# One PSUM bank moved from the down projection to the convolution, results taken out one operation at a time, and other shares of work per unit

## The chip, the cores and the metric

The kernel runs on one core of one Trainium2 chip. The metric is device time in microseconds (us) of one execution, as a median of several; executions of one kernel agree here within about 0.2% (0.34% in one run). The engines are PE (matmul), PEld (its weight loads), DVE (vector), ACT (scalar), POOL (GpSimd) and SP, which only issues transfers. PSUM is the memory that PE writes its results to; the kernel uses it as eight banks.

## The reference

```python
h_filt = (np.maximum(pos_emb @ w1, 0.0) @ w2) * np.exp(-0.01 * pos)[:, None]
u = x * v                                        # (4, 12480, 128)
y = irfft(rfft(u, 2*S) * rfft(h_filt, 2*S))[:, :S]   # a causal convolution per channel
t = (x * y).reshape(49920, 128)
h = t @ w_in                                     # 128 -> 2048
return (h * np.cos(h)) @ w_out                   # 2048 -> 128
```

All is float32. The long convolution is done as matmuls in two passes there and two back.

## The kernel before

A convolution of one batch element has five stages. **u** forms x times v and its sums and differences, without PE. **f1** and **f2** are the two transforms there, and f2's result is multiplied with the filter's spectrum. **i1** and **i2** are the two transforms back. Every stage is a Python generator of "units" (30 in u, 64 in f1, 48 in f2, 64 in i1, 30 in i2). A unit's matmuls go to a PSUM bank, and `after` takes the bank's content out one unit later:

```python
    def units(n, steps, before, mm, after, ahead=2):
        for j in range(min(ahead, n)):
            before(j)
        last = None
        for j in range(n):
            if j + ahead < n:
                before(j + ahead)
            now = mm(j)
            if last is not None:
                after(j - 1, last)
            last = now
            yield steps
        after(n - 1, last)
        yield REST

    U_STEPS, F1_STEPS, F2_STEPS, I1_STEPS, I2_STEPS = 2.1, 1.2, 2.3, 1.2, 1.6

    def f2_product(pool, ps, h, k1):
        ...
        for r, op in ((0, ALU.subtract), (1, ALU.add)):
            nc.vector.tensor_tensor(y[:, r], uu[:, 0], hh[:, r], op=ALU.mult)
            nc.vector.tensor_tensor(t[:, r], uu[:, 1], hh[:, 1 - r], op=ALU.mult)
            nc.gpsimd.tensor_tensor(y[:, r], y[:, r], t[:, r], op=op)

    def u_multiply(tiles, engine):
        xt, vt = tiles
        engine.tensor_tensor(xt[:, :, :], xt[:, :, :], vt[:, :, :], op=ALU.mult)

    def u_sums(u, tiles, a):
        ...
        for place, op, e in ((a, ALU.add, nc.gpsimd), (ODD + a, ALU.subtract, nc.vector)):
            e.tensor_tensor(u[...], below, above, op=op)
```

The cosine layer runs in 1664 "steps" (104 tiles of 480 tokens, 16 chunks of hidden width each). A step is an up matmul into bank `ph`, then a (ACT), k (DVE), f (POOL), cs (ACT), gt (DVE), then a down matmul that adds into bank `acc`. The down matmul trails by four steps. The first convolution runs alone at the start; the other three are threaded into the first 1140 steps, each unit being given its number of steps:

```python
        ps_acc = ctx.enter_context(tc.tile_pool(name="ps_acc", bufs=2, space=PSUM))
        ps_h = ctx.enter_context(tc.tile_pool(name="ps_h", bufs=4, space=PSUM))
        ps_c = ctx.enter_context(tc.tile_pool(name="ps_c", bufs=2, space=PSUM))
        ...
        for i in range(len(steps) + LAG):
            if i < len(steps):
                ...
                hidden[i] = moe_up(mpool, n, c)               # PE, ACT a, DVE k, POOL f
            if 0 <= i - 1 < len(steps):
                gates[i - 1] = moe_act(mpool, *hidden.pop(i - 1))   # ACT cs, DVE gt
            if i >= LAG:
                moe_down(pn, pc, gates.pop(i - LAG))          # PE
                if pc == NFC - 1:
                    ots[pn] = moe_evict(mpool, pn)            # ACT ot <- acc
            ...
            owed += share
            while owed > 0.0:
                owed -= next(conv, owed)                      # units of the convolution
```

## Time and profile before

| | before |
|---|---|
| median (runs) | 4256.94 us (4256.48 to 4257.34) |
| start, until the first up matmul | 635 us |
| steps with three convolutions threaded in | 2742 us |
| steps alone (tail), to the last up matmul | 874 us |

The three parts are read from the profiled execution, whose span was 4262.5 us; 11 us follow the last up matmul.

Three of the page's costliest groups: line, engine, operation, output from inputs, shapes and count, then busy time and mean ns of one, then idle time just before them and what ended it.

```profile
L578 POOL TENSOR_TENSOR f<-a,k 128x480 f32<-128x480 f32 x1664 | 2021.9, 1218 | 1174.9 <-DVE k L575 1174.9
L569 PE MATMUL ph<-at,w_in_sb 128*128 128x480 f32 x3328 | 1647.4, 577 | 102.6 <-DVE gt L585 101.6
L369 POOL TENSOR_TENSOR slots<-slots,t 120x256 f32<-120x256 f32 x384 | 296.6, 795 | 228.2 <-DVE t L368 176.6
```

PE waits 102 us at the up matmul for gt, which frees a ph bank. POOL waits for DVE's products of f2 (t, L368) for 177 us. Both waits belong to the threaded stretch or the start; the tail has no gap.

Throughout this document a stage's **loss** is its length minus what its matmuls cost PE back to back. I count the matmuls in the stage's stretch and take 0.4007 us for each of the two instructions of an up or down matmul, 0.161 in f1, 0.2135 in f2, 0.1005 in i1, 0.107 in i2, and 0.11 for a transpose. These are start-to-start times in full stretches of the timeline; the medians over the whole trace are up to 3% higher, which would take some 12 us off the sum. In the tail the same costs leave 3 us of 874. A loss holds both PE's waits and the time lost while the granted clock was low. It is read from one profiled execution of each kernel. Over three convolutions the kernel before loses u 122, f1 21, f2 123, i1 22, i2 14 us.

### The profile page before, as it was taken

Reading aid. Unit: us, or ns where it says so; the run is one execution under the profiler, and the core shown is the slowest. Engines: PE = TensorE matmul, PEld = TensorE weight load, DVE = VectorE, ACT = ScalarE, POOL = GpSimd, SP = SyncE. Lnnn points to the kernel's source line nnn. Section 1 sums busy time; section 2 is a strip of 40 time slices with the busy share of each in tenths; the row PEclk is TensorE's granted clock in tenths of the full one; section 3 lists DMA queues with packets and bytes.
Section 4 is the critical chain, followed back from the end, with each engine's and each line's share of the span. In section 5 each row is a group of like instructions: output and inputs, shape, how many; then the busy total and the mean of one; then the engine's idle time right before and its main releaser. Section 6 shows DMA issues by size and latency. Waiting matters only on the chain.

```text
span 4262.5 us, 49170 instructions
## 1 busy us (share of the span) xinstructions
PE 3916.4 (92%) x13882; PEld 2244.3 (53%) x13882; DVE 3047.8 (72%) x6588; ACT 2415.2 (57%) x4484; POOL 2546.8 (60%) x2311
## 2 busy tenths in 40 slices
PE   5868778999999998998899989988999999999999
PEld 3836673554456653554466634644466644444444
DVE  8657669987778568777776588766675566666666
ACT  1343155775567445655455456644554577777777
POOL 2422347657865457568854476568754577777776
PEclk8557889999999999999999999999999999999999
DMA  3354343112211442012201531022103400000000
GB/s 86 89 167 120 96 136 106 50 52 78 82 51 42 142 142 85 15 50 81 75 12 51 177 112 42 15 73 78 52 15 107 127 19 19 19 19 19 19 19 14
DMA packets 271763, 293.63 MB, mean 69 GB/s; under 512 B 16741, under 2 KB 204101, under 8 KB 271237
## 3 DMA queue, kind: packets, MB, share of 16 engines
q1 hardware_dynamic: 271493, 290.50, 23.6%
q8 instruction: 112, 1.84, 0.2%
q14 instruction: 158, 1.29, 0.1%
HBM read 210.12 MB, written 80.31 MB: 68 GB/s over the span
## 4 chain that ended last, share of the span: by engine, by line
PE 65%; POOL 11%; DVE 10%; ACT 5%; DMA 5%; issue 3%; SPq 0%; DVEq 0%; POOLq 0%; ACTq 0%
PE ph L569 24%; PE acc L591 23%; POOL f L578 6%; POOL slots L369 5%; PE cv L404 4%; PE cv L386 4%; ACT cs L583 3%; PE cv L343 3%; PE ps L343 3%; DVE gt L585 2%; DMA w<-wd 2%; DMA hd<-h 2%; PE ph L116 2%; DVE slots L336 1%; PE ps L386 1%
## 5 line engine op out<-in xcount | busy, mean ns | idle before, releaser
L578 POOL TENSOR_TENSOR f<-a,k 128x480 f32<-128x480 f32 x1664 | 2021.9, 1218 | 1174.9 <-DVE k L575 1174.9
L569 PE MATMUL ph<-at,w_in_sb 128*128 128x480 f32 x3328 | 1647.4, 577 | 102.6 <-DVE gt L585 101.6
L591 PE MATMUL acc<-gt,w_out_sb 128*128 128x480 f32 x3328 | 1618.0, 568 | 0.5 <-DVE gt L585 0.5
L572 ACT ACTIVATE a<-ph,quarter 128x480 f32<-128x480 f32 x1664 | 1094.2, 658 | 750.7 <-PE ph L569 691.8
L585 DVE TENSOR_TENSOR gt<-ph,cs 128x480 f32<-128x480 f32 x1664 | 1091.7, 656 | 476.3 <-ACT cs L583 452.7
L583 ACT ACTIVATE cs<-f 128x480 f32<-128x480 f32 x1664 | 998.4, 600 | 690.6 <-POOL f L578 688.7
L575 DVE TENSOR_SCALAR k<-a 128x480 f32<-128x480 f32 x1664 | 778.8, 468 | 528.3 <-ACT a L572 514.4
L591 PEld LDWEIGHTS acc<-gt,w_out_sb 128*128 128x128 f32 x3328 | 633.8, 190 | 715.5 <-issue 713.5
L569 PEld LDWEIGHTS ph<-at,w_in_sb 128*128 128x128 f32 x3328 | 584.8, 191 | 575.4 <-issue 290.4
L369 POOL TENSOR_TENSOR slots<-slots,t 120x256 f32<-120x256 f32 x384 | 296.6, 795 | 228.2 <-DVE t L368 176.6
L357 PE MATMUL ps<-slots,w 124*120 124x256 f32 x384 | 165.9, 576 | 80.7 <-DVE w L250 45.6
L386 PEld LDWEIGHTS cv<-cs,slots 120*96 120x96 f32 x1536 | 180.5, 168 | 82.0 <-issue 72.1
L357 PE MATMUL cv<-slots,w 124*120 124x256 f32 x576 | 155.3, 390 | 49.7 <-PE acc L591 36.0
L404 PEld LDWEIGHTS cv<-slots,tm 96*104 96x104 f32 x1440 | 173.1, 171 | 46.7 <-issue 36.0
L386 PE MATMUL cv<-cs,slots 120*96 120x120 f32 x1536 | 191.2, 267 | 3.3 <-POOL slots L369 3.3
L404 PE MATMUL cv<-slots,tm 96*104 96x128 f32 x1440 | 178.7, 275 | 11.0 <-DMA tm<-td 7.2
L343 PEld LDWEIGHTS cv<-c,slots 104*124 104x124 f32 x768 | 130.6, 192 | 84.4 <-issue 54.8
L357 PEld LDWEIGHTS ps<-slots,w 124*120 124x120 f32 x384 | 93.0, 268 | 153.0 <-issue 70.5
L357 PEld LDWEIGHTS cv<-slots,w 124*120 124x120 f32 x576 | 98.7, 182 | 134.3 <-PE acc L591 78.0
L343 PE MATMUL cv<-c,slots 104*124 104x192 f32 x768 | 159.5, 330 | 3.2 <-POOL slots L336 2.6
L396 DVE TENSOR_TENSOR slots<-cv,other 96x240 f32<-96x240 f32 x384 | 135.9, 393 | 0.5
L330 POOL TENSOR_TENSOR xt<-xt,vt 104x512 f32<-104x512 f32 x30 | 38.3, 1276 | 137.5 <-DMA vt<-in_v_dram 127.0
(111 smaller groups left out, 2781.8 us busy)
## 6 DMA issues: line engine op xcount, KB each, us to landing
h<-hd SPq DMA_DIRECT2D x192, 240.0 KB
tm<-td SPq DMA_DIRECT2D x90, 312.0 KB
xt<-in_x_dram SPq DMA_DIRECT2D x120, 208.0 KB
vt<-in_v_dram SPq DMA_DIRECT2D x120, 208.0 KB
xs<-in_x_dram SPq DMA_DIRECT2D x120, 208.0 KB
zd<-zs SPq DMA_DIRECT2D x120, 208.0 KB
zb<-zd SPq DMA_DIRECT2D x104, 240.0 KB
out_dram<-ob SPq DMA_DIRECT2D x104, 240.0 KB
```

The source lines that it names most:

```text
L343: nc.tensor.matmul(ps[0:KE, i * 2 * N1:(i + 1) * 2 * N1], u[:, b, 0:KE, i], c1[0:u.shape[0], :, :].rearrange("p r k -> p (r k)"), start=Tr ...
L357: nc.tensor.matmul(ps[0:N2, i * 2 * D:(i + 1) * 2 * D], w[:, i, :], parts[0:KE, :, k1 + i, :, :], start=True, stop=True)
L369: nc.gpsimd.tensor_tensor(y[:, r], y[:, r], t[:, r], op=op)
L386: nc.tensor.matmul(ps[0:N1, (i * 2 + r) * N2:(i * 2 + r + 1) * N2], parts[0:N2, r, :, b, i], cs[:, r:r + 2, :].rearrange("p c a -> p (c a) ...
L404: nc.tensor.matmul(ps[0:R, i * D:(i + 1) * D], t[:, i, r, :], slots[0:N1, :, place, :], start=(r == 0), stop=(r == 1))
L569: nc.tensor.matmul(ph[:, 0:TOK], w_in_sb[:, c * P:(c + 1) * P], ats[n][:, :], start=True, stop=True)
L572: nc.scalar.activation(a[:, :], ph[:, 0:TOK], AF.Identity, bias=quarter[:, 0:1], scale=INV_TWO_PI)
L575: nc.vector.tensor_scalar(out=k[:, :], in0=a[:, :], scalar1=ROUND, scalar2=ROUND, op0=ALU.add, op1=ALU.subtract)
L578: nc.gpsimd.tensor_tensor(f[:, :], a[:, :], k[:, :], op=ALU.subtract)
L583: nc.scalar.activation(cs[:, :], f[:, :], AF.Sin, scale=TWO_PI)
L585: nc.vector.tensor_tensor(gt[:, :], ph[:, 0:TOK], cs[:, :], op=ALU.mult)
L591: nc.tensor.matmul(accs[n][:, 0:TOK], w_out_sb[:, c, :], gt[:, :], start=(c == 0), stop=(c == NFC - 1))
```

## The change

It is meant to let PE run on while results are taken out. The convolution gets a third bank, paid for by the second bank of the down sums; in the tail, where the convolution banks lie idle, odd tiles borrow one. The results of a unit are no longer taken out in one burst: `after` is a generator now, and each of its pieces is followed by a share of a unit's steps; a unit's matmuls are issued in two halves as well. u and f2 get more steps per unit, f1 and i1 fewer. Two copies out of PSUM move from DVE to ACT, and every third row of a table is made with POOL. The transposes of a tile move, so that four of them stand between the last down matmul of one tile and the first of the next.

```diff
-    def units(n, steps, before, mm, after, ahead=2):
+    def units(n, steps, before, mm, after, parts, ahead=2):
...
-            now = mm(j)
-            if last is not None:
-                after(j - 1, last)
-            last = now
-            yield steps
-        after(n - 1, last)
+            now = None
+            for i in range(parts):
+                if i == 0 or 2 * i == max(parts, 2):
+                    now = mm(j, now, min(i, 1))
+                if i == 0 and parts == 1:
+                    now = mm(j, now, 1)
+                next(last, None)
+                yield steps / parts
+            next(last, None)
+            last = after(j, now)
+        for _ in last:
+            pass
         yield REST
...
-    U_STEPS, F1_STEPS, F2_STEPS, I1_STEPS, I2_STEPS = 2.1, 1.2, 2.3, 1.2, 1.6
+    U_STEPS, F1_STEPS, F2_STEPS, I1_STEPS, I2_STEPS = 2.75, 0.8, 2.9, 0.8, 1.6
...
             nc.vector.tensor_tensor(y[:, r], uu[:, 0], hh[:, r], op=ALU.mult)
+            yield
             nc.vector.tensor_tensor(t[:, r], uu[:, 1], hh[:, 1 - r], op=ALU.mult)
             nc.gpsimd.tensor_tensor(y[:, r], y[:, r], t[:, r], op=op)
+            yield
...   (the same in f1_evict, i1_evict, i2_out and filter_keep; u multiplies in two halves)
-        nc.vector.tensor_copy(out=at[:, :], in_=pt[:, 0:TOK])
+        nc.scalar.copy(out=at[:, :], in_=pt[:, 0:TOK])
...   (the same for ob; the transposes move to other steps of a tile)
-            accs[n] = ps_acc.tile([P, BANK], F32, name="acc")
+            accs[n] = bank() if ready == B - 1 and n % 2 else \
+                ps_acc.tile([P, BANK], F32, name="acc")
...
-        ps_acc = ... bufs=2 ...
+        ps_acc = ... bufs=1 ...
-        ps_c = ... bufs=2 ...
+        ps_c = ... bufs=3 ...
```

More of the change, by code (lines that the diff above doesn't have):

```diff
@@ L268, in make_t, with make_third @@
              tw_t[:, 1, n2:n2 + 1], **how)
+    def make_third(pool, t, n2, half=None):
+        if n2 % 3 < 2:
+            make_t(t, n2, half=half)
+        else:
+            spare = pool.tile([N1, 2, R], F32, name="spare")
+            make_t(t, n2, spare=spare[:, :, :])
     ROWS = 8
@@ L326, in u_load, with u_multiply @@
         return tiles
-    def u_multiply(tiles, engine):
+    def u_multiply(tiles, half, engine):
         xt, vt = tiles
-        engine.tensor_tensor(xt[:, :, :], xt[:, :, :], vt[:, :, :], op=ALU.mult)
+        engine.tensor_tensor(xt[:, half, :], xt[:, half, :], vt[:, half, :], op=ALU.mult)
     def u_sums(u, tiles, a):
@@ L337, in u_sums, with f1_mm @@
                             below, above, op=op)
-    def f1_mm(ps, u, b):
-        for i in range(2):
-            nc.tensor.matmul(ps[0:KE, i * 2 * N1:(i + 1) * 2 * N1], u[:, b, 0:KE, i],
-                             c1[0:u.shape[0], :, :].rearrange("p r k -> p (r k)"),
-                             start=True, stop=True)
+    def f1_mm(ps, u, b, i):
+        nc.tensor.matmul(ps[0:KE, i * 2 * N1:(i + 1) * 2 * N1], u[:, b, 0:KE, i],
+                         c1[0:u.shape[0], :, :].rearrange("p r k -> p (r k)"),
+                         start=True, stop=True)
     def f1_evict(ps, b):
@@ L350, in f1_evict, with f2_mm @@
         nc.vector.tensor_copy(out=parts[ODD:KE, 0, :, b, :], in_=pj[ODD:KE, 1])
+        yield
         nc.vector.tensor_scalar(out=parts[ODD:KE, 1, :, b, :], in0=pj[ODD:KE, 0],
                                 scalar1=-1.0, scalar2=None, op0=ALU.mult)
-    def f2_mm(ps, w, k1):
-        for i in range(2):
-            nc.tensor.matmul(ps[0:N2, i * 2 * D:(i + 1) * 2 * D], w[:, i, :],
-                             parts[0:KE, :, k1 + i, :, :], start=True, stop=True)
+        yield
+    def f2_mm(ps, w, k1, i):
+        nc.tensor.matmul(ps[0:N2, i * 2 * D:(i + 1) * 2 * D], w[:, i, :],
+                         parts[0:KE, :, k1 + i, :, :], start=True, stop=True)
     def f2_product(pool, ps, h, k1):
@@ L367, in f2_product @@
             nc.vector.tensor_tensor(y[:, r], uu[:, 0], hh[:, r], op=ALU.mult)
+            yield
             nc.vector.tensor_tensor(t[:, r], uu[:, 1], hh[:, 1 - r], op=ALU.mult)
             nc.gpsimd.tensor_tensor(y[:, r], y[:, r], t[:, r], op=op)
+            yield
     def filter_keep(pool, ps, h, k1):
@@ L380, in filter_keep, with i1_mm @@
                     in1=h[:, g, r, :], op0=ALU.mult, op1=ALU.add)
+            yield
         nc.sync.dma_start(hd[k1 // 2, :, :, :, :], h[:, :, :, :])
-    def i1_mm(ps, b):
-        for i in range(2):
-            for r in range(2):
-                nc.tensor.matmul(
-                    ps[0:N1, (i * 2 + r) * N2:(i * 2 + r + 1) * N2],
-                    parts[0:N2, r, :, b, i],
-                    cs[:, r:r + 2, :].rearrange("p c a -> p (c a)"), start=True, stop=True)
+    def i1_mm(ps, b, i):
+        for r in range(2):
+            nc.tensor.matmul(
+                ps[0:N1, (i * 2 + r) * N2:(i * 2 + r + 1) * N2],
+                parts[0:N2, r, :, b, i],
+                cs[:, r:r + 2, :].rearrange("p c a -> p (c a)"), start=True, stop=True)
     def i1_evict(pool, ps, b):
@@ L397, in i1_evict, with i2_mm @@
                                     other[:, :, :], op=op)
-    def i2_mm(ps, t, g):
-        for i in range(G):
+            yield
+    def i2_mm(ps, t, g, part):
+        for i in range(part * G // 2, (part + 1) * G // 2):
             n2 = g * G + i
@@ L415, in i2_out @@
         nc.sync.dma_start(zd[b, :, g * G:(g + 1) * G, :], zs[:, :, :])
-    def units(n, steps, before, mm, after, ahead=2):
+        yield
+    def units(n, steps, before, mm, after, parts, ahead=2):
         for j in range(min(ahead, n)):
             before(j)
-        last = None
+        last = iter(())
         for j in range(n):
@@ L445, in before, with after, mm @@
                 tiles[j] = u_load(pool, bufs, b, j * UA)
-            def mm(j):
-                u_multiply(tiles[j], engine)
-                return tiles.pop(j)
+            def after(j, _):
+                for half in range(2):
+                    u_multiply(tiles[j], half, engine)
+                    yield
+                u_sums(u, tiles.pop(j), j * UA)
+                yield
             clear_gap(u)
-            yield from units(H // UA, U_STEPS, before, mm,
-                             lambda j, t: u_sums(u, t, j * UA), ahead=bufs - 2)
+            yield from units(H // UA, U_STEPS, before, lambda j, ps, i: None, after, 3,
+                             ahead=bufs - 2)
     def f1_units(bank, u):
-        def mm(j):
-            ps = bank()
-            f1_mm(ps, u, j)
+        def mm(j, ps, i):
+            if i == 0:
+                ps = bank()
+            f1_mm(ps, u, j, i)
             return ps
-        return units(CB, F1_STEPS, lambda j: None, mm, lambda j, ps: f1_evict(ps, j))
+        return units(CB, F1_STEPS, lambda j: None, mm, lambda j, ps: f1_evict(ps, j), 2)
     def f2_units(bank, use, make=None):
@@ L479, in before, with mm @@
                     nc.sync.dma_start(hs[j][:, :, :, :], hd[j, :, :, :, :])
-            def mm(j):
-                ps = bank()
-                f2_mm(ps, ws.pop(j), 2 * j)
+            def mm(j, ps, i):
+                if i == 0:
+                    ps = bank()
+                f2_mm(ps, ws[j], 2 * j, i)
                 return ps
             yield from units(N1 // 2, F2_STEPS, before, mm,
-                             lambda j, ps: use(pool, ps, hs.pop(j), 2 * j))
+                             lambda j, ps: use(pool, ps, hs.pop(j), 2 * j),
+                             4 if use is f2_product else 2)
     def i1_units(bank):
         with tc.tile_pool(name="mid", bufs=2) as pool:
-            def mm(j):
-                ps = bank()
-                i1_mm(ps, j)
+            def mm(j, ps, i):
+                if i == 0:
+                    ps = bank()
+                i1_mm(ps, j, i)
                 return ps
             yield from units(CB, I1_STEPS, lambda j: None, mm,
-                             lambda j, ps: i1_evict(pool, ps, j))
+                             lambda j, ps: i1_evict(pool, ps, j), 2)
     def i2_units(bank, b, make=None):
@@ L512, in before, with mm @@
                                   block(x, b, slice(j * G, (j + 1) * G)))
-            def mm(j):
-                ps = bank()
-                i2_mm(ps, ts.pop(j), j)
+            def mm(j, ps, i):
+                if i == 0:
+                    ps = bank()
+                i2_mm(ps, ts[j], j, i)
                 return ps
             yield from units(N2 // G, I2_STEPS, before, mm,
-                             lambda j, ps: i2_out(pool, ps, xss.pop(j), b, j))
+                             lambda j, ps: i2_out(pool, ps, xss.pop(j), b, j), 2)
     def t_units():
@@ L527, in t_units @@
                 for i in range(G):
-                    make_t(t[:, i, :, :], g * G + i)
+                    make_third(pool, t[:, i, :, :], g * G + i)
                     yield
@@ L535, in conv_units @@
         keep = t_units() if b == 1 else iter(())
-        for steps in f1_units(bank, slots[0:R, :, :, :]):
-            next(keep, None)
+        for i, steps in enumerate(f1_units(bank, slots[0:R, :, :, :])):
+            if i % 2:
+                next(keep, None)
             yield steps
         yield from f2_units(bank, f2_product)
-        for steps in i1_units(bank):
-            next(keep, None)
+        for i, steps in enumerate(i1_units(bank)):
+            if i % 2:
+                next(keep, None)
             yield steps
@@ L603, in moe_store @@
         ob = pool.tile([N2, TOK // N2, D], F32, name="ob", bufs=1)
-        nc.vector.tensor_copy(out=ob[:, :, :].rearrange("i m d -> i (m d)"),
-                              in_=pt[0:N2, :])
+        nc.scalar.copy(out=ob[:, :, :].rearrange("i m d -> i (m d)"), in_=pt[0:N2, :])
         nc.sync.dma_start(
@@ L667 @@
             for j, _ in enumerate(f1_units(bank, slots[0:FR, :, :, :])):
-                if j % 4 == 3:
+                if j % 8 > 4:
                     next(first_u, None)
@@ L671 @@
                     bank, filter_keep, lambda w, k1: make_w(w, k1, half=bank))):
-                if j % 3 == 2:
+                if j % 2:
                     next(first_u, None)
@@ L690 @@
             with tc.tile_pool(name="spare", bufs=2) as pool:
-                def make(t, n2):
-                    if n2 % G < G - 1:
-                        make_t(t, n2, half=bank)
-                    else:
-                        spare = pool.tile([N1, 2, R], F32, name="spare")
-                        make_t(t, n2, spare=spare[:, :, :])
-                for _ in i2_units(bank, 0, make):
+                for _ in i2_units(bank, 0, lambda t, n2: make_third(pool, t, n2, bank)):
                     pass
-        ps_acc = ctx.enter_context(tc.tile_pool(name="ps_acc", bufs=2, space=PSUM))
+        ps_acc = ctx.enter_context(tc.tile_pool(name="ps_acc", bufs=1, space=PSUM))
         ps_h = ctx.enter_context(tc.tile_pool(name="ps_h", bufs=4, space=PSUM))
-        ps_c = ctx.enter_context(tc.tile_pool(name="ps_c", bufs=2, space=PSUM))
+        ps_c = ctx.enter_context(tc.tile_pool(name="ps_c", bufs=3, space=PSUM))
         mpool = ctx.enter_context(tc.tile_pool(name="moe", bufs=2))
@@ L747 @@
             if i < len(steps):
-                if c == LAG + 1 and n - 1 in ots:
+                if c == LAG - 1 and n + 1 < NALL:
+                    moe_turn(mpool, n + 1)
+                if c == NFC // 2 and n - 1 in ots:
                     moe_store(mpool, n - 1, ots.pop(n - 1))
-                if c == NFC // 2 and n + 1 < NALL:
-                    moe_turn(mpool, n + 1)
             owed += share
```

## The prediction

> **What bounds the kernel now.** The page comes first, and in it the strip of slices: how busy each engine is along the run.
>
> ```profile
> PE   5868778999999998998899989988999999999999
> DVE  8657669987778568777776588766675566666666
> POOL 2422347657865457568854476568754577777776
> PEclk8557889999999999999999999999999999999999
> ```
>
> Slices are 107 us. Up to slice 6 (about 640 us) the filter and the first convolution run; then come 1664 "steps" of the cosine layer (up matmul, a, k, f, cs, gt, down matmul), with convolutions 1 to 3 threaded into the first 1140 of them, and the last 524 alone. PE is at 9 everywhere but in dips that come three times. To name them I asked for busy time in stretches of 100 us; columns: PE, PEld, DVE, ACT, POOL, granted clock, DMA share, GB/s.
>
> ```profile
> 1300.00:1400.00 100.00, 100.00 (x478) 62.79 (x477) 80.38 (x191) 69.39 (x152) 50.61 (x42) 1.00 0.15 41
> 1600.00:1700.00 100.00, 82.01 (x208) 34.48 (x206) 90.18 (x139) 53.78 (x94) 76.09 (x66) 1.00 0.29 88
> 1900.00:2000.00 100.00, 90.64 (x264) 46.23 (x264) 71.14 (x162) 48.80 (x85) 81.69 (x80) 1.00 0.30 82
> 3500.00:3600.00 100.00, 100.00 (x270) 48.35 (x269) 69.65 (x128) 76.55 (x126) 72.56 (x61) 1.00 0.06 15
> ```
>
> The first line is stage i1 and the last is the tail: PE full. The second is stage u (x times v, sums and differences), the third stage f2 (product with the filter). Only these two leave PE free.
>
> How much they lose: the tail runs 481 steps in 800 us (count of f in the groups of that stretch), so a step with its share of transposes costs PE 1.663 us. By the starts in the timeline, one f1 unit adds 0.65 us of PE, f2 0.85, i1 0.80, i2 1.71. Cutting the run where matmuls of one source line stop and the next begin, stage u of convolution 2 (1550 to 1694 us) holds 63.5 steps: 144 minus 106 leaves 38 us lost; f2 (1866 to 2130) holds 112 steps and 48 units: 264 minus 186 minus 41 leaves 37. Over three convolutions u loses about 118 us, f2 126 (40, 37, 49), and f1, i1, i2 together some 50, of which perhaps half is error of my unit costs. The prize is therefore at most 250 to 290 us, 6 to 7%.
>
> Why u loses: the timeline of DVE there,
>
> ```profile
> 1599.20 0.85 DVE L330 TENSOR_TENSOR xt<-xt,vt 104x512 f32<-104x512 f32 x1
> 1599.97 0.95 DVE L336 TENSOR_TENSOR slots<-xt 104x256 f32<-104x256 f32 x1
> 1600.84 0.40 DVE L575 TENSOR_SCALAR k<-a 128x480 f32<-128x480 f32 x1
> 1601.16 0.65 DVE L585 TENSOR_TENSOR gt<-ph,cs 128x480 f32<-128x480 f32 x1
> 1601.73 1.05 DVE L575 TENSOR_SCALAR k<-a 128x480 f32<-128x480 f32 x1
> ```
>
> and of POOL:
>
> ```profile
> 1599.46 1.17 POOL L336 TENSOR_TENSOR slots<-xt 104x256 f32<-104x256 f32 x1
> 1601.32 1.20 POOL L578 TENSOR_TENSOR f<-a,k 128x480 f32<-128x480 f32 x1 [0.68 <-DVE k L575]
> 1602.86 1.20 POOL L578 TENSOR_TENSOR f<-a,k 128x480 f32<-128x480 f32 x1 [0.35 <-DVE k L575]
> 1604.02 1.18 POOL L336 TENSOR_TENSOR slots<-xt 104x256 f32<-104x256 f32 x1
> ```
>
> k takes 0.40 us when POOL is still and 1.05 when POOL runs f; DVE's L336 takes 0.41 or 0.95 likewise. They take turns. One unit with two steps lasts 4.56 us (1599.46 to 1604.02), all of it turns of f, k, multiply (0.53 undisturbed), add on POOL (0.66) and subtract (0.33). So a step costs this turn-taking 1.51 us (4.56 minus 1.52, halved) and the unit 1.5.
>
> Why f2 loses: there DVE does four products in one burst, and the waits show PE held at its next convolution matmul (the releaser printed is PE's own older matmul; the products' end fits, 1959.27 against a start at 1959.36).
>
> ```profile
> PE cv L357 <- PE acc L591: 12.1, 17, 0.8
> PE ph L569 <- DVE gt L585: 10.5, 14, 1.1
> ```
>
> [...] 0.40 against 1.05 us above; gt, with an input in PSUM, keeps 0.65. [...]
>
> **The change part by part.**
> (1) Third convolution bank, and DVE's operations handed out one per chunk. It aims at f2. Before, a steady f2 unit takes 50 us/9.3 units = 5.38 us against 4.68 of PE (2.3 x 1.663 + 0.85). Turn-taking would allow about 2.3 x 1.51 + 2 x 0.69 = 4.85 (0.69 is my estimate of L369 without k's share, on the line through f, 480 elements in 1.20, and L255, 208 in 0.62); so 0.5 us per unit is burst and bank wait. After, with 2.9 steps, PE needs 4.82 + 0.85 = 5.67 and turn-taking 2.9 x 1.51 + 1.38 = 5.76. Adding 0.1 to 0.3 us of remaining disorder, a unit loses 0.2 to 0.4 us: 29 to 58 us for 144 units, against 144 x 0.70 = 101 before. Saved: 43 to 72, say 62.
> (2) u gets 2.75 steps for 2.1. PE needs 4.57 per unit; turn-taking 2.75 x 1.51 + 1.65 = 5.80 (the multiply in halves costs 2 x 0.33 instead of 0.53). Lost per unit 1.23. Before: 2.1 x 1.51 + 1.52 = 4.69, less 3.49 of PE, is 1.20. So u gains nothing: 0, or 3 us worse.
> (3) f1 and i1 get 0.8 steps for 1.2. Both stay on PE (1.33 + 0.65 = 1.98 us a unit; DVE's two operations and 0.8 steps are some 1.5). All stages together keep 380 steps a convolution (379.6/382.5 of planned steps, and the share is scaled by the same sum), so this only shifts steps: 0.
> (4) Copies at and ob (104 each, 0.65 and 0.68 us) leave DVE for ACT, 57% busy. In the tail nothing waits for either: 0. In u and f2 (some 36 tiles) each sat in front of a k: about 0.25 us a tile, 8 us saved.
> (5) One bank for down sums while convolutions run. The next tile's first down matmul must wait for the ACT copy ot. In the timeline at 1748 the copy ended 1748.64 and that matmul began 1749.10, and now four transposes lie between too, so in f1, i1, i2 it is hidden. In u and f2 the copy stands behind a cs that lags; PE will wait 1 to 3 us per tile, but POOL has two f in hand meanwhile; I charge 0.3 us x 36 = 11 us lost. The tail alternates two banks: 0.
> (6) A third of the table rows to POOL (L253 0.80 and L255 0.62 us, 40 times) in f1/i1 of convolution 1, where POOL is half idle: 0. The start before 640 us is paced by its own loads (160 to 170 GB/s, POOL waiting for vt): 0, give or take 8. Third bank at stage borders in f1, i1, i2: 10 saved.
> Sum: 62 - 3 + 8 - 11 + 10 = 66 saved; I lean to the upper side, 72, because hand-tuned shares usually fit better than my sum. 4257 - 72 = **4185 us**.
>
> **Rivals.** A: the bank and the bursts were the whole trouble, and turn-taking is looser than I read it. Then u and f2 both go to PE's pace: up to 200 us, 4060 to 4100. For it: DVE at 90% in u loses two copies and its bursts. Against: the 4.56 us cycle has no free turn. B: the single sum bank becomes the wait in place of the one removed: PE loses its lead once per tile in 71 tiles; at 1 us each 71 us, and the change is worth nothing, 4250. For it: the copy queues behind cs, whose waits for POOL reach 4.3 us. Against: PE is not what u and f2 wait for. C: ACT becomes the bound in f1 of convolution 1 (copy, table row, a, cs: some 2.5 us of durations per step against PE's 2.48). Durations overlap by about 0.1 us, so I count 2.1; if wrong, 20 us worse, 4205.
>
> **Range and chances.** My sum's weak terms are f2's disorder (30 us either way), the sum bank (-10 to +50) and u (-40 to +10). 8 in 10: 4120 to 4235. Faster by over 2% means below 4172: a little under half. Slower than 4342 has no mechanism I can size.
>
> **What would show it.** Tail steps at 1.66 us again; moe start near 640. f2 stretches with PE at 95% or more and the wait of L357's successor gone; if PE stays at 90%, step 1 is wrong. u stretches with PE near 80% still and k still near 0.68 us on average; PE at 90% there means rival A [...]. New waits of the acc matmul on ACT's ot, a few us per tile only in u and f2; the same in f1 and i1 would be rival B. ACT over 95% in f1 of convolution 1 would be C.

## The result

The changed kernel takes 4147.1 us (4143.61 to 4150.47, four runs) against 4257.14 of the kernel before in the same rounds. The ratio is 0.974 (95% interval 0.9723 to 0.9757), so it is 2.6% faster. A ratio here is the mean time of one kernel's fast runs over that of the other's of the same rounds, so it is not quite the ratio of the medians quoted.

The strip of slices of the changed kernel (a slice is 104 us now; the kernel before is in the prediction):

```profile
PE   5958788899999998999999999999999999999999
DVE  8657678997888569878876599778765566666666
POOL 2521556777886457558864477488744577777776
PEclk7567799999999999999999999999999999999999
```

The dips of PE are down to single slices. Stretches that answer to those of before (PE, PEld, DVE, ACT, POOL, clock, DMA share, GB/s) are i1, u, f2 and the tail:

```profile
1250.00:1350.00 100.00, 100.00 (x541) 67.60 (x540) 84.56 (x199) 74.32 (x175) 66.48 (x67) 1.00 0.18 52
1600.00:1700.00 100.00, 89.15 (x206) 38.62 (x207) 94.38 (x144) 58.01 (x102) 75.24 (x65) 0.92 0.27 77
1900.00:2000.00 100.00, 98.28 (x294) 52.04 (x293) 82.50 (x168) 64.90 (x109) 86.06 (x85) 1.00 0.27 78
3500.00:3600.00 100.00, 100.00 (x274) 48.59 (x273) 65.62 (x120) 79.16 (x132) 72.24 (x61) 1.00 0.07 20
```

In f2 PE went from 90.64% with 264 matmuls to 98.28% with 294. In u the busy share rose from 82 to 89%, but the matmuls did not: 206 against 208. A lower clock stretched them, which the column 0.92 says. The busy share alone would mislead here.

The waits of PE in f2 of convolution 2 (engine, tile, line, what it waited for: us in all, times, longest):

```profile
PE acc L622 <- ACT ot L627: 3.3, 7, 0.7
PE cv L365 <- ACT a L601: 0.5, 1, 0.5
```

The 12.1 us at the convolution's matmul and the 10.5 us at the up matmul are gone. A new wait of 3.3 us has come, for the copy that frees the single sum bank. In u of the same convolution, DVE's timeline (start and duration in us; in brackets, the idle time before and what ended it):

```profile
1600.53 1.38 DVE L338 TENSOR_TENSOR xt<-xt,vt 104x256 f32<-104x256 f32 x1
1601.84 0.40 DVE L604 TENSOR_SCALAR k<-a 128x480 f32<-128x480 f32 x1
1602.30 0.66 DVE L614 TENSOR_TENSOR gt<-ph,cs 128x480 f32<-128x480 f32 x1
1602.88 0.92 DVE L338 TENSOR_TENSOR xt<-xt,vt 104x256 f32<-104x256 f32 x1
```

The halves of the multiply, half the elements of before, take longer than the whole did (0.85 us): DVE arrives at them while POOL works, and the row includes the time until POOL lets go: in u of this convolution 52 of the 60 halves start while a POOL instruction runs, and each of the 52 ends 0.28 to 0.29 us after that instruction. PE there:

```profile
1600.67 1.07 PE L598 MATMUL ph<-at,w_in_sb 128*128 128x480 f32 x2 [1.25 <-DVE gt L614]
1602.77 1.97 PE L622 MATMUL acc<-gt,w_out_sb 128*128 128x480 f32 x2 [1.03 <-ACT ot L627]
1604.53 1.81 PE L598 MATMUL ph<-at,w_in_sb 128*128 128x480 f32 x2
```

After two waits of over 1 us in a row, a pair of matmuls takes 1.8 to 2.0 us instead of 1.0. The granted clock was 0.50 from 1602.0, 0.3 us into the second wait, to 1608.9, although PE was busy without a gap for the last 6.1 us of it. No run here isolates what brings it down. In u as a whole, over three convolutions, PE's waits fell from 73 to 54 us, but the time lost to a lower clock rose from 12 to 22 (summed over the traces' waits and clock records). That is part of why u gained so little.

Losses by stage, summed over the three convolutions, for the two kernels and for all twelve experiments. Times are medians; each ratio is to the kernel before on the same chip in the same rounds. The column "start" is when the first up matmul began in the trace; it varies from 633 to 642 us without regard to the kernel, so I compare the losses where a few us matter. The entries of a row are rounded singly and can differ from its sum by 2.

| kernel | us | ratio | start | u | f1 | f2 | i1 | i2 | sum |
|---|---|---|---|---|---|---|---|---|---|
| before | 4257 | 1 | 635 | 122 | 21 | 123 | 22 | 14 | 302 |
| changed | 4147 | 0.974 | 637 | 116 | 16 | 31 | 19 | 7 | 187 |
| x3_before_banks | 4269 | 1.0023 | 636 | 128 | 16 | 126 | 22 | 15 | 306 |
| x5_before_steps | 4319 | 1.014 | 635 | 124 | 63 | 94 | 68 | 11 | 360 |
| x9_whole_units | 4212 | 0.9884 | 634 | 124 | 9 | 95 | 17 | 8 | 253 |
| x1_old_banks | 4534 | 1.0648 | 638 | 109 | 185 | 112 | 158 | 8 | 571 |
| x2_conv2_acc1 | 4543 | 1.0663 | 635 | 116 | 183 | 110 | 154 | 7 | 569 |
| x4_old_steps | 4157 | 0.9759 | 642 | 124 | 17 | 16 | 19 | 11 | 187 |
| x6_copies_dve | 4166 | 0.9781 | 638 | 115 | 17 | 40 | 19 | 7 | 198 |
| x7_v_psum | 4093 | 0.9612 | 633 | 69 | 12 | 30 | 13 | 7 | 131 |
| x8_u_noport | 4071 | 0.9559 | 638 | 39 | 13 | 30 | 17 | 7 | 105 |
| x10_noport_old_steps | 4081 | 0.9577 | 641 | 54 | 13 | 15 | 18 | 12 | 113 |
| x11_noport_mid | 4086 | 0.9589 | 633 | 58 | 13 | 25 | 19 | 10 | 125 |
| x12_noport_f2_old | 4077 | 0.9572 | 640 | 46 | 16 | 19 | 22 | 13 | 114 |

The sum falls by 115 us from before to changed; the medians fall by 110, and the two profiled executions differ by 114 (4262.5 and 4148.7). The gain is f2 (92 us), then small pieces: i2 7, u 6, f1 5, i1 3.

### The profile page after: what moved, and what is told of

It is laid out like the page before. It is cut to its first block, busy times and chain, and to the rows that moved or that the text cites.

```text
span 4148.7 us, 49336 instructions
## 1 busy us (share of the span) xinstructions
PE 3885.9 (94%) x13882; PEld 2254.5 (54%) x13882; DVE 3050.5 (74%) x6420; ACT 2534.8 (61%) x4692; POOL 2614.4 (63%) x2441
## 4 chain that ended last, share of the span: by engine, by line
PE 70%; POOL 10%; DVE 7%; DMA 5%; ACT 4%; issue 3%; SPq 0%; POOLq 0%; DVEq 0%; ACTq 0%
PE ph L598 25%; PE acc L622 20%; POOL f L607 7%; PE cv L622 5%; PE cv L415 4%; PE cv L396 4%; PE ps L350 3%; PE cv L365 2%; PE cv L350 2%; ACT cs L612 2%; DMA w<-wd 2%; DVE k L604 2%; PE ph L116 2%; POOL slots L344 1%; DMA hd<-h 1%
## 5 line engine op out<-in xcount | busy, mean ns | idle before, releaser
L622 PE MATMUL acc<-gt,w_out_sb 128*128 128x480 f32 x2784 | 1364.7, 572 | 16.7 <-ACT ot L627 16.2
L622 PEld LDWEIGHTS acc<-gt,w_out_sb 128*128 128x128 f32 x2784 | 527.8, 191 | 631.3 <-issue 577.1
L378 POOL TENSOR_TENSOR slots<-slots,t 120x256 f32<-120x256 f32 x384 | 306.0, 803 | 139.0 <-DVE t L377 132.9
L622 PE MATMUL cv<-gt,w_out_sb 128*128 128x480 f32 x544 | 263.2, 566 | 0.5 <-DVE gt L614 0.5
L338 DVE TENSOR_TENSOR xt<-xt,vt 104x256 f32<-104x256 f32 x180 | 189.7, 1064 | 0.0
L365 PE MATMUL cv<-slots,w 124*120 124x256 f32 x576 | 173.7, 382 | 7.0 <-DMA w<-wd 6.1
L622 PEld LDWEIGHTS cv<-gt,w_out_sb 128*128 128x128 f32 x544 | 103.2, 190 | 116.7 <-issue 114.5
```

The source lines that it names most:

```text
L365: nc.tensor.matmul(ps[0:N2, i * 2 * D:(i + 1) * 2 * D], w[:, i, :], parts[0:KE, :, k1 + i, :, :], start=True, stop=True)
L622: nc.tensor.matmul(accs[n][:, 0:TOK], w_out_sb[:, c, :], gt[:, :], start=(c == 0), stop=(c == NFC - 1))
```

## The experiments

The theory at this point was that f2's burst and its bank were mended, and that u is still bound by POOL and DVE taking turns. The rivals were that a single part of the change (bank, steps) is the whole gain, and that u is bound by something else. All twelve kernels gave correct results.

### x1_old_banks and x2_conv2_acc1: is the third bank needed?

```diff
# x1: the changed kernel with 2 sum banks and 2 convolution banks
-            accs[n] = bank() if ready == B - 1 and n % 2 else \
-                ps_acc.tile([P, BANK], F32, name="acc")
+            accs[n] = ps_acc.tile([P, BANK], F32, name="acc")
-        ps_acc ... bufs=1     ps_c ... bufs=3
+        ps_acc ... bufs=2     ps_c ... bufs=2
# x2: the changed kernel with ps_c bufs=2 only
```

> The changed kernel with the PSUM banks of before: two for the down sums, two for the convolution; chunks and steps as changed. Theory (the third convolution bank is what makes the spread-out products work: with two banks a unit's first matmul needs the products of two units before, whose last one is issued only one chunk, 0.7 of a step, earlier): f2 loses its gain again, 60 to 100 us, and the u stages gain 10 to 20 us from the second sum bank; 4195 to 4235 us in all, and waits of L365 on cv come back. Rival 1 (the spreading of the products alone did it, the bank is spare): 4130 to 4150 us. Rival 2 (the single sum bank costs much): below 4120 us.

> The changed kernel with one sum bank, four ph banks and only two convolution banks (one bank unused). Against the changed kernel it isolates the third convolution bank, against x1_old_banks the single sum bank. Theory: 15 us slower than x1_old_banks (4210 to 4250 us), all of that in u and f2, where the next tile's first down matmul waits for the copy of the sums; loss of f2 as in x1_old_banks. Rival 1 (bank is spare): equal to the changed kernel, 4147 us. Rival 2 (single sum bank dear): 40 us or more above x1_old_banks.

Measured: 4534 and 4543 us, 6.5% slower than the kernel before. The third bank is needed at the new steps, but the size and the place were far off what I wrote: of the 384 us by which the losses exceed the changed kernel's, most lies in f1 (169) and i1 (139), and 81 in f2. The timeline of PE in f1 of x1 shows how:

```profile
1902.02 0.57 PE L350 MATMUL cv<-c,slots 104*124 104x192 f32 x2 [1.29 <-DVE slots L359]
1902.42 0.97 PE L598 MATMUL ph<-at,w_in_sb 128*128 128x480 f32 x2
1903.23 0.97 PE L621 MATMUL acc<-gt,w_out_sb 128*128 128x480 f32 x2
1904.04 0.49 PE L350 MATMUL cv<-c,slots 104*124 104x192 f32 x2
1905.82 0.89 PE L350 MATMUL cv<-c,slots 104*124 104x192 f32 x4 [1.29 <-DVE slots L359]
```

and of DVE:

```profile
1904.20 0.41 DVE L604 TENSOR_SCALAR k<-a 128x480 f32<-128x480 f32 x1 [2.05 <-ACT a L601]
1904.64 0.66 DVE L614 TENSOR_TENSOR gt<-ph,cs 128x480 f32<-128x480 f32 x1
1905.31 0.36 DVE L359 TENSOR_SCALAR slots<-cv 60x192 f32<-60x192 f32 x1
```

PE waits 1.29 us for L359, the last operation on the bank it wants. L359 stands in DVE's queue behind k, and k waits 2.05 us for a, which waits for an up matmul that PE has not started, because PE stands before the f1 matmul. Each engine waits for the other, and PE's lead over DVE is lost. Over the three convolutions PE waits for L359 106 times, 134.7 us in all, and for the like operation of i1 (L406) 108 times, 117.3 us. With spread operations, a bank's last operation is issued only 0.4 of a step before the bank is wanted again; with three banks it is a whole unit more.

x2 against x1 should also have told what the single sum bank costs. It did not: the intervals of the two ratios (1.0632 to 1.0664, 1.0647 to 1.0679) overlap. In u alone the losses are 109 and 116 us, and with two sum banks the stretch of u in convolution 2 held 4 us at a clock below 0.9 (in slices of 2 us) against 12 with one. So some 7 us, in u, is what these two traces say; x3 below shows a case in which the single bank costs far more.

### x3_before_banks, x5_before_steps, x9_whole_units: each part without the spreading

```diff
# x3: the kernel before with 1 sum bank and 3 convolution banks, nothing else
# x5: the kernel before with 2.75, 0.8, 2.9, 0.8, 1.6 steps, nothing else
# x9: the kernel before with those banks, those steps, the copies on ACT and the
#     transposes moved; units still handed out whole
```

> The kernel before with nothing changed but the banks: one for down sums (two in turn in the tail), three for the convolution. Theory: PE no longer waits at L357 for a cv bank (36 us of waits before), but DVE still does four products in one burst, so POOL still waits for them: f2 gains 20 to 50 us, the sum bank costs 10 to 20 in u and f2; 4215 to 4250 us. Rival 1 (the bank alone is the whole gain): 4150 to 4170 us. Rival 3 (neither helps without the other): 4255 to 4270 us.

> The kernel before with only the steps per unit of the changed one (2.75, 0.8, 2.9, 0.8, 1.6). Theory, from x1_old_banks and x4_old_steps: a bank's next matmul waits for products issued that many steps earlier, and with two banks 0.8 steps are too few, so f1 and i1 lose 0.2 to 0.5 us a unit on 384 units and f2 keeps its burst loss; 4300 to 4420 us. Rival (rebalancing is harmless or good alone): 4230 to 4260 us.

> Everything of the change but the spreading: the kernel before, with the new banks, the new steps, the copies on ACT and the new places of the transposes, but units still handed out whole, with DVE's operations in one burst. Theory: the third bank mends f1 and i1 at 0.8 steps (loss about 20 us each, against 63 and 68 in x5_before_steps), while f2 keeps the burst loss of x5_before_steps (94 us, against 31 in the changed kernel) and u stays turn-bound at some 118; 4195 to 4230 us. Rival (with three banks the burst no longer matters, spreading is for nothing): f2 loss under 45 us, 4140 to 4165 us.

Measured: 4269, 4319 and 4212 us. Moving the bank alone gains nothing (ratio 1.0023): not what I expected, but the time of the rival "neither helps without the other". f2's loss stays at 126. PE's waits over the whole run show why, first of the kernel before, then of x3:

```profile
PE ph L569 <- DVE gt L585: 101.6, 173, 1.9
PE cv L357 <- PE acc L591: 36.0, 54, 0.8
```

```profile
PE acc L592 <- ACT ot L597: 78.2, 34, 3.4
PE ph L569 <- DVE gt L585: 66.4, 131, 2.7
```

The third convolution bank did its work: the 36 us at L357 are gone and the wait for gt fell by 35. The single sum bank took as much back: 78 us for the copy ot, 49 of them in f2 and 28 in u. The mean clock in the three f2 stages fell as well, to 0.97, 0.97 and 0.94 from 0.99, 1.00 and 0.99. So x3 shows the prediction's rival B, and it does not test a third bank by itself; no run gives the convolution a third bank and leaves the sums two. In x9 the wait for ot is 20.3 us, in the changed kernel 16.2. x9 differs from x3 in the steps, the copies and the places of the transposes; the four transposes that now stand between two tiles' sums are the likely reason, but no run isolates them.

The steps alone cost 1.4%: f1 and i1 at 0.8 steps lose 63 and 68 us with two banks, and f2 loses 29 less than before. My range for x5 (4300 to 4420) held.

x9 came as expected: with three banks f1 and i1 are mended (9 and 17 us), f2 keeps its burst loss (95 against 31). x9 also lacks the table rows on POOL, which belong to f1 and i1. Spreading the operations, with these rows, is then worth 4212 - 4147 = 65 us (61 by the ratios), and 64 of the losses' 66 lie in f2, where PE's wait for gt falls from 34 us to none. At the old steps the same shows: from x3 to x4 (next section) f2's loss falls from 126 to 16, with the copies and the transposes in it too. So neither the moved bank nor the steps gain alone, and the spreading loses without the third bank at the new steps (x1). The spreading alone, with two banks and the old steps, was not run.

### x4_old_steps: the rebalancing

```diff
# the changed kernel
-    U_STEPS, F1_STEPS, F2_STEPS, I1_STEPS, I2_STEPS = 2.75, 0.8, 2.9, 0.8, 1.6
+    U_STEPS, F1_STEPS, F2_STEPS, I1_STEPS, I2_STEPS = 2.1, 1.2, 2.3, 1.2, 1.6
```

> The changed kernel with the old steps per unit (2.1, 1.2, 2.3, 1.2, 1.6). Theory: in f2 at 2.3 steps turn-taking between POOL and DVE needs about 4.85 us a unit against 4.68 of PE, so f2 loses 0.2 to 0.35 us a unit more than at 2.9; u is turn-bound either way; 10 to 25 us slower than the changed kernel: 4157 to 4175 us. Rival 4 (the rebalancing is what the change is worth): 4200 to 4240 us.

Measured: 4156.77 us, inside my range, but not for my reason. f2 loses less at 2.3 steps (16 us) than at 2.9 (31); u loses 8 more. The sums of the losses are the same, 187. Of the 10 us, 5 lie in the start, which differs by as much between runs of like kernels. So the rebalancing has no gain that these runs can show. f2's 16 us are also less than my turn-taking allows: 4.85 us a unit against 4.68 of PE would lose at least 24.

### x6_copies_dve: the copies

```diff
# the changed kernel
-        nc.scalar.copy(out=at[:, :], in_=pt[:, 0:TOK])
+        nc.vector.tensor_copy(out=at[:, :], in_=pt[:, 0:TOK])
# and the same for ob
```

> The changed kernel with the copies at and ob on DVE again. Theory: in the tail, f1, i1, i2 and now f2 nothing waits for them; in u they sit in front of a k: 3 to 15 us slower than the changed kernel, 4150 to 4162 us, all in u. Rival (DVE, 97% busy in u, is the bound there, and the copies count in full): 25 us or more slower, u longer by 0.65 us per copy.

Measured: 4165.86 us, 19 us slower than the changed kernel by the medians of two series, 11 by the losses. It is more than I wrote, and 9 of the 11 lie in f2, none in u. A likely reading, which no run here isolates, is that in f2 the copy on DVE delays a product or a k that POOL wants at once. In f2 PE's wait for gt rises from none to 3.2 us there, and that for ot from 7.6 to 10.5.

### x7_v_psum and x8_u_noport: what binds u

In x7, ACT copies v into a convolution bank that u does not use, so the multiply reads one operand from PSUM. In x8, the second half of the product stays in PSUM too, and both sums run on DVE with one PSUM operand each; POOL's add is gone.

```diff
+                xt, vt = tiles.pop(j)
+                pv = bank()
+                nc.scalar.copy(out=pv[0:R, :], in_=vt[:, :, :].rearrange("p h c -> p (h c)"))
+                w = UA * D
+                nc.vector.tensor_tensor(xt[:, 0, :], xt[:, 0, :], pv[0:R, 0:w], op=ALU.mult)
+                yield
+                nc.vector.tensor_tensor(pv[0:R, w:2 * w], xt[:, 1, :], pv[0:R, w:2 * w],
+                                        op=ALU.mult)
+                yield
+                below = xt[:, 0, :].rearrange("p (n b i) -> p n b i", n=UA, i=2)[:, ::-1, :, :]
+                above = pv[0:R, w:2 * w].rearrange("p (n b i) -> p n b i", n=UA, i=2)
+                for place, op in ((j * UA, ALU.add), (ODD + j * UA, ALU.subtract)):
+                    nc.vector.tensor_tensor(
+                        u[0:R, :, place:place + UA, :].transpose([0, 2, 1, 3]),
+                        below, above, op=op)
```

> The changed kernel, but in the u stages of convolutions 1 to 3 ACT first copies v into a free convolution bank, so that DVE's multiply has one SBUF input and one PSUM input and no longer takes turns with POOL (results the same). Theory (u is bound by turn-taking): two turns of 0.33 us less in each of 90 units, u units from 5.98 us to about 5.3; 4085 to 4105 us, multiply at 0.41 us instead of 1.06. Rival (DVE's own time or the order of its queue, or the sum bank, binds u): the multiply itself gets no shorter than its undisturbed time, 4140 to 4165 us.

> As x7_v_psum, and the second half of the product stays in PSUM, so that sum and difference both run on DVE with one PSUM input each; nothing of u takes turns with POOL any more. Theory: turns 2.75 x 1.51 = 4.15 us a unit, PE 4.57 and DVE about 2.75 x 0.9 + 4 x 0.33 = 3.8, so u comes down to PE: its loss of 116 us falls to 15 to 35, 4040 to 4070 us. Rival (DVE is the bound in u): two sums instead of one on DVE make it worse than x7_v_psum.

Measured: 4093.45 us (ratio 0.9612) and 4070.97 us (0.9559), x7 inside the range of the theory and x8 1 us above it (4040 to 4070). u loses 69 and then 39 us instead of 116; for x8 I had expected 15 to 35, so something in u stays unexplained. The instructions that touch tile xt on DVE in u of convolution 2, with ns minimum, median and maximum of one: the kernel before and the changed kernel, then x7, then x8 (the two sums).

```profile
L330 DVE TENSOR_TENSOR xt<-xt,vt x30: 693/854/978, 1554.4 to 1689.9; 104x512 f32<-104x512 f32 x30
L338 DVE TENSOR_TENSOR xt<-xt,vt x60: 410/950/1390, 1526.4 to 1696.2; 104x256 f32<-104x256 f32 x60
```

```profile
L339 DVE TENSOR_TENSOR xt<-xt,cv x60: 403/410/422, 1504.4 to 1657.2; 104x256 f32<-104x256 f32 x60
L345 DVE TENSOR_TENSOR slots<-xt x30: 584/746/985, 1508.0 to 1657.6; 104x256 f32<-104x256 f32 x30
```

```profile
L486 DVE TENSOR_TENSOR slots<-xt,cv x60: 411/415/421, 1504.2 to 1645.3; 104x256 f32<-104x256 f32 x60
```

The same multiply on the same number of elements falls from a median of 950 ns to 410, and its spread from 980 ns to 19, when one operand moves to PSUM. In x7 the subtraction, still with two operands in SBUF, still spreads from 584 to 985; in x8 it is steady too. With the ends 0.28 us after POOL's, this settles what the extra time in the DVE rows was: waiting for POOL. DVE itself has more work in x8 (two sums instead of one) and yet the stage is shorter, which rules out the rival that DVE's own time binds u. POOL has less work in x8, so x7, which moves one operand and leaves POOL's work as it was, is the cleaner test of the turns. In x8 no 2 us slice of u in convolution 2 has a clock below 0.9; the changed kernel has 16 us of them.

### x10_noport_old_steps, x11_noport_mid, x12_noport_f2_old: other steps on top of x8

Each is x8_u_noport with another line of steps: 2.1, 1.2, 2.3, 1.2, 1.6, then 2.3, 1.0, 2.5, 1.0, 1.6, then 2.75, 1.1, 2.3, 1.1, 1.6.

> x8_u_noport with the old steps per unit (2.1, 1.2, 2.3, 1.2, 1.6). In x4_old_steps f2 lost 16 us at 2.3 steps, less than 31 at 2.9, and u no longer takes turns, so it does not need many steps. Theory: f2 gains 10 to 15 us, u at 2.1 steps has PE 3.49 and DVE about 3.2 us a unit and loses 5 to 15 us more; 4055 to 4075 us, equal to x8_u_noport within 0.5%. Rival (u needs its 2.75 steps because DVE is nearly as full as PE): u loses 40 us or more against x8_u_noport, 4100 us or more.

> x8_u_noport with steps between (2.3, 1.0, 2.5, 1.0, 1.6). Theory: as x10_noport_old_steps or a few us better, 4050 to 4070 us; the sum of steps hardly matters once no stage is turn-bound. Rival: as there, 4085 us or more.

> x8_u_noport with u at 2.75 steps and f2 back at 2.3, f1 and i1 at 1.1 (2.75, 1.1, 2.3, 1.1, 1.6). Theory: the losses by stage of the other runs add up (u 39 us as in x8_u_noport, f2 16 as in x4_old_steps and x10_noport_old_steps, the rest 35 to 45): 4050 to 4065 us, a few tenths of a per cent faster than x8_u_noport. Rival (losses move from one stage to the next when steps are shifted): 4070 to 4085 us.

Measured: 4081, 4086 and 4077 us. None beats x8_u_noport at 4071; the intervals of x8, x10 and x12 overlap. The ranges of the theory were missed by 6 (x10), 16 (x11) and 12 us (x12), and x11 and x12 lie in those of their rivals: losses do not add up from run to run, they move. In x12, f2 falls to 19 as hoped, while f1, i1, i2 and u take back 21 together. These three shifts gained nothing. x8_u_noport is the version that beats both kernels: 4.4% under the kernel before.

## Why the prediction was right or wrong

The time of 4185 us was 38 us too high; 4147 lies in the range of 4120 to 4235, and "faster by over 2%" had been given a little under half. Of the 72 us forecast, 66 came from the sum and 6 from a lean to the upper side that no mechanism carried; that the lean pointed the right way is luck.

1. *"It aims at f2 ... Saved: 43 to 72, say 62."* The mechanism was right, and the term was under-sized: f2 saved 92 us. The loss before was not 101 but 123. The prediction had counted 126 itself, by cutting the run into stages, and then used 0.70 us of a steady stretch for every unit, which leaves out the borders and convolution 3's slow units. With its own 126 the term would have been 68 to 97, and 92 lies within. The loss left was 31, at the low end of "29 to 58". x4 speaks against the turn-taking sum for f2, which forbids the 16 us measured there; what sets the rest of f2's loss stays open. (The 0.69 us in it is low too: the line through its two points gives 0.72.) What the step did not see is that the moved bank alone gains nothing (x3), that spreading at the new steps loses without it (x1), and that the third bank matters most in f1 and i1 at 0.8 steps.
2. *"So u gains nothing: 0, or 3 us worse."* Right: 122 to 116. The turn-taking of POOL and DVE is shown by x7 and x8. The unit was to take 5.80 us of turns; u of convolution 2 took about 180 us (1518 to 1698) for 30 units, 6.0 each. (Two slips of the sum hardly matter: 4.56 minus 1.52, halved, is 1.52, and the undisturbed multiply, for which I had estimated 0.53, is 0.69 in the shortest row, about 0.6 without the overlap of rows; the shortest half is 0.41, so in these rows two halves, 0.82, do cost more than the whole.) Two of my signs for it failed. The average of k fell from 0.68 us to about 0.43, because the multiply now does the waiting (each half averages 1.06 us and takes 0.41 in the shortest row); and PE looked 89% busy, which I had named as the sign of rival A, but at a clock of 0.92 and with no more matmuls. Counting matmuls would have been the right sign.
3. *"Both stay on PE ... 0."* Held with three banks: f1 and i1 lose 16 and 19. It does not hold with two (x5: 63 and 68), so this step rested on the bank without saying so.
4. *"8 us saved"* by the copies: 11 to 19, in f2, not in u.
5. *"0.3 us x 36 = 11 us lost"* for the single sum bank: about 7 us in u; the whole is not resolved (x1 against x2). PE's wait for ot is 16.2 us in 31 waits in the page of the changed kernel, practically all in u and f2, as foreseen. The part not foreseen is the clock, which was at 0.50 for 7 us around one such wait.
6. Borders: 10 us foreseen; f1, i1 and i2 together gained 15. The table rows on POOL, "0, give or take 8", have no run of their own; the first up matmul began at 637 us against 635.

Rival A (u at PE's pace) did not happen; x8 comes near it, with 39 us still lost. Rival B's wait came, at a fraction of 1 us a tile on average; in x3, where the bank is moved and nothing else, it came in full (78 us). Rival C did not show: ACT was busy for 82% of f1 of convolution 1, not over 95, and that stage lost 10 us against 8 before.

The sum in the prediction was 62 - 3 + 8 - 11 + 10. As the losses have it, f2 with the copies' share saved 92, u with the sum bank's share 6, and f1, i1, i2 together 15. So most of the miss is the term for f2; u, where a net loss was foreseen, and the other stages give the rest.

## What to carry to other kernels

Before spreading the work on a result over time, count how long before the next use of its buffer the last piece is now issued: in x1 it was 0.4 of a step, the piece stood behind a k in DVE's queue, and DVE and PE waited for each other. Here the moved buffer gained nothing alone, spreading without it, at the new steps, lost 6.5%, and together they paid. When a buffer is taken from one place for another, look for the wait that the giver gets: in x3 it took back all that was won. And when a stage's loss has been measured whole, use that figure, not a steady stretch times the number of units. When DVE and POOL are both at work, look at the spread of a row's durations: in u the multiply's minimum of 410 ns, far below its median of 950, meant that it waited for POOL inside its row. With one operand copied to PSUM by ACT, which was 60% busy in u, its median was 410 ns too, and the kernel took 54 us less of 4147 (x7). Compare the count of matmuls per stretch, not only the busy share: in u PE went from 82 to 89% busy with 206 matmuls for 208, at a clock of 0.92 instead of 1.00.
